# The last two batches' channel layers in one 2x2 block scheme with seven products

## The chip, the cores and the metric

The kernel runs on one core of one Trainium2 chip. The metric is the device time of one launch in microseconds (us), the median of several runs. Engines are named as the profile names them: PE is the matrix engine (PEld its weight load), DVE the vector engine, ACT the scalar engine, POOL the GpSimd engine, SP the engine whose queue issues most DMAs.

## The reference

Eight batches, twelve heads, 448 rows, head size 64. Cosine attention feeds a token mixer and a channel mixer:

```python
q_n = q / (norm(q) + 1e-06); k_n = k / (norm(k) + 1e-06)
attn = softmax(q_n @ k_n.T / tau)               # per batch and head
x = (attn @ v) as (8, 448, 768)
h  = relu(x.T @ w_tok1) @ w_tok2                # 448 -> 256 -> 448, over rows
u  = x + h.T
h2 = relu(u @ w_ch1) @ w_ch2                    # 768 -> 1536 -> 768, over channels
out = u + h2
```

The channel layers are the two matrix products of the last but one line. They work row by row, so two batches of 448 rows are simply 896 rows under the same weights.

## The kernel before

Matrix operands are fp16, sums are fp32 in PSUM. The work is cut into 48 pairs of heads, six pairs for each batch. The main loop runs over the pairs `i`; its order is written out by hand and nothing reorders it. In one turn of the loop, called a segment here, PE does for pair `i` the scores (`score`, `score_rest`), for pair `i-1` the product with v (`pv_rest`, `pv`) and the first token layer (`tok1`), and for pair `i-2` the second token layer (`tok2`). ACT does the exponentials out of PSUM. DVE divides (`rec`, `x`), adds the residual (`u`), and reduces the squares (`ssq`). POOL squares, scales and casts the inputs that come next (`side`). SP issues loads, stores and two DMA transposes for each pair: `tpose_dma` for the scaled q and k of pair `i+2`, and `udma`, which turns `u16` into `ut`, the operand of the first channel layer.

The channel layers are cut into units on a list (`queue`). A unit of `m_ch1` is one 128-channel tile of the hidden layer: six matmuls of 448 columns into one PSUM bank, then one ACT relu into `gt`. A unit of `m_ch2` is twelve matmuls of 384 columns, one DVE add of `u16`, and stores. An even batch has 12 + 6 units, an odd one 12 + 8, since the last 64 rows of an even batch share a 128-row tile with the first 64 of the odd one. When the third pair of batch `b` comes up, `refill(b - 1)` puts the units of the batch before on the list, and `due` hands them out so that they spread over the next six segments. They fill PE's waits. After the last segment the rest of batch 6 runs, mixed with the last pair's steps, then all of batch 7.

PSUM has two pools: `ps` with two buffers of one bank (tag "b"), `ps2` with three buffers of two banks (tag "s"). A wait is set for each tile: a matmul into a tile waits for the readers of the tile, even where they read its other bank.

Of the kernel before, what the change touches and what calls it, by code (L numbers as in the profile page):

```python
# [7 lines left out]
FP32 = mybir.dt.float32  # L8
FP16 = mybir.dt.float16
AF = mybir.ActivationFunctionType  # L10
ALU = mybir.AluOpType
# [11 lines left out]
def kernel(  # L23
# [12 lines left out]
    nc = tc.nc  # L36

    B, H, S, E = q.shape
    D = H * E
    T = moe_w_tok1.shape[1]  # L40
    C = moe_w_ch1.shape[1]
    SC = 112
    NCH = S // SC
    DT = D // 128
    CT = C // 128
    TT = T // 128
    DH = 384
    NPAIR = H // 2
    NP_ALL = B * NPAIR
    HP = 3  # L50
# [12 lines left out]
    KC = 3  # L63
    KS = 2 * KC + 1
    QS = 2 * NCH
    MAIN = [(128 * m, 128 * (m + 1)) for m in range(3)]
# [3 lines left out]
    def windows(b):  # L70
        return EVEN if b % 2 == 0 else ODD

    def pieces(lo, hi):
        got = []
        while lo < hi:
            c = lo // SC
            end = min(hi, SC * (c + 1))
            got.append((c, lo - SC * c, end - SC * c))
            lo = end
        return got  # L80

    cst = ctx.enter_context(tc.tile_pool(name="cst", bufs=1))
    qkv = ctx.enter_context(tc.tile_pool(name="qkv", bufs=7))
    nrm = ctx.enter_context(tc.tile_pool(name="nrm", bufs=3))
    att = ctx.enter_context(tc.tile_pool(name="att", bufs=4))
    mix = ctx.enter_context(tc.tile_pool(name="mix", bufs=2))
    outp = ctx.enter_context(tc.tile_pool(name="outp", bufs=3))
    ps = ctx.enter_context(tc.tile_pool(name="ps", bufs=2, space=bass.MemoryType.PSUM))
    ps2 = ctx.enter_context(tc.tile_pool(name="ps2", bufs=3, space=bass.MemoryType.PSUM))

# [2 lines left out]
    ut = {}  # L93
    u16 = {}
    gts = {}

    def old(i):
        return i < OLD


    def load_first(a, src):
# [3 lines left out]
                          in_=src[0, g].rearrange("(p c) e -> p (c e)", c=NCH))  # L105
        return t

    def load_rows(i, nm, src, bufs):
        h0 = 2 * (i % NPAIR)
        if old(i):  # L110
            t = qkv.tile([SC, QS, E], FP32, name=f"{nm}f_{i}", tag=f"{nm}f", bufs=bufs)
            nc.sync.dma_start(
                out=t[:].rearrange("p (g c) e -> p g (c e)", g=2),
                in_=src[h0:h0 + 2].rearrange("g (p c) e -> p g (c e)", c=NCH))
            return t
        t = qkv.tile([128, 2 * KC, E], FP32, name=f"{nm}f_{i}", tag=f"{nm}f", bufs=bufs)
        nc.sync.dma_start(out=t[:].rearrange("p (g c) e -> p g (c e)", g=2),
                          in_=src[h0:h0 + 2, 0:128 * KC].rearrange("g (p c) e -> p g (c e)", c=KC))
        return t

    def load_rest(i, nm, src):
        h0 = 2 * (i % NPAIR)
        t = qkv.tile([128, HP, E], FP32, name=f"{nm}r_{i}", tag=f"{nm}r", bufs=4)
        for g in range(2):
            nc.sync.dma_start(out=t[64 * g:64 * g + 64],
                              in_=src[h0 + g:h0 + 2 * HP:2, 128 * KC:S].rearrange("j p e -> p j e"))
        return t
# [29 lines left out]
    wc1t = cst.tile([128, DT, C], FP16, name="wc1t")  # L157
    wc2t = cst.tile([128, CT, D], FP16, name="wc2t")
# [1 line left out]
    NV = 3  # L160
    vts = []
    for i in range(NV):
        vt = cst.tile([128, HP, QS, E + 2], FP16, name=f"vt{i}")
        nc.gpsimd.memset(vt[:, :, :, E:E + 2].rearrange("p g c e -> p (g c) e"), 1.0)
        vts.append(vt)
    pts = []
    for i in range(2):
        pt = cst.tile([128, QS * S + 64], FP16, name=f"pt{i}")
        nc.gpsimd.memset(pt[:, QS * S:QS * S + 64], 0.0)
        nc.gpsimd.memset(pt[96:128, KS * S:KS * S + 64], 0.0)  # L170
        pts.append(pt)
# [32 lines left out]

    kqs = [cst.tile([128, 2, NCH, 2, E], FP16, name=f"kq{i}") for i in range(4)]
    sqs = [cst.tile([128, 2 * QS, E], FP32, name=f"sq{i}") for i in range(3)]
    for kq in kqs:
        nc.vector.memset(kq[96:128, 1].rearrange("p c g e -> p (c g e)"), 0.0)  # L210

# [39 lines left out]
    def some(i, a0, a1):  # L251
        sl, np_ = lay(i)
        return max(np_[a0:a1]), slice(sl[a0].start, sl[a1 - 1].stop)

    def sums(i, a0=0, a1=2):
        n, sl = some(i, a0, a1)
        st = pipe[i]
        if "ssq" not in st:
            st["ssq"] = nrm.tile([128, 2 * QS], FP32, name=f"ssq_{i}", tag="ssq", bufs=4)
            st["rn"] = nrm.tile([128, 2 * QS], FP32, name=f"rn_{i}", tag="rn", bufs=4)  # L260
        nc.vector.tensor_reduce(out=st["ssq"][0:n, sl], in_=st["sq"][0:n, sl], axis=AXX.X, op=ALU.add)  # L261
# [158 lines left out]
    def tok2(i, pe=False, wide=False):  # L420
        st = pipe[i]
        b, pj = i // NPAIR, i % NPAIR
        if pj == 0:
            u16[b] = mix.tile([128, DT, 4, 128], FP16, name=f"u16_{b}", tag="u16", bufs=4)
            ut[b] = mix.tile([128, DT, 4, 128], FP16, name=f"ut_{b}", tag="ut")
        psU = (ps2 if wide else ps).tile([128, 4, 128], FP32, name=f"psU_{i}", tag="s" if wide else "b")
        for m, lo in enumerate(windows(b)):
            for tt in range(TT):
                nc.tensor.matmul(psU[:, m], w2t[:, tt, lo:lo + 128], st["rt"][:, tt],  # L429
                                 start=(tt == 0), stop=(tt == TT - 1))  # L430
        u = u16[b][:, pj]
        nc.vector.tensor_tensor(out=u, in0=psU[:], in1=st["x"][:], op=ALU.add)  # L432
        if not pe:
            udma(i)

    def udma(i):
        b, pj = i // NPAIR, i % NPAIR
        nc.sync.dma_start_transpose(out=ut[b][:, pj], in_=u16[b][:, pj].rearrange("p m d -> p (m d)"))

    def upose(i, n=1):  # L440
        b, pj = i // NPAIR, i % NPAIR
        psT = ps.tile([128, n, 4, 128], FP16, name=f"psT_{i}", tag="b")
        for j in range(n):
            for m in range(4):
                nc.tensor.transpose(psT[:, j, m], u16[b][:, pj + j, m], id16[:])
        nc.vector.tensor_copy(out=ut[b][:, pj:pj + n], in_=psT[:])
# [20 lines left out]
    ost = {}  # L467
# [40 lines left out]
    def ch1_units(b):  # L508
        return [(ns(S, DT), lambda wide, ct=ct: m_ch1(b, ct, wide)) for ct in range(CT)]

    def ch2_units(b):
# [6 lines left out]
        else:  # L518
            order = [(m, c) for m in range(3) for c in cuts]
            if b % 2:  # L520
# [2 lines left out]
        return [(ns(hi - lo, CT), lambda wide, m=m, lo=lo, hi=hi, st=st: m_ch2(b, m, lo, hi, st, wide))  # L523
                for m, (lo, hi, st) in order]

    queue = []
    fed = [0.0, 0.0]

    def unit(wide=False):
        if queue:  # L530
            t, fn = queue.pop(0)
            fn(wide)
            fed[0] -= t

    def due():
        return queue and fed[0] > queue[0][0] / 2

    KEPT = 6000.0

    def refill(b):  # L540
        new = ch1_units(b) + ch2_units(b)
        fed[1] = (sum(t for t, _ in new) - (KEPT if b == 0 else 0.0)) / (NPAIR + 1 if b == 0 else NPAIR)
        queue.extend(new)

    with tc.manual_schedule():
# [3 lines left out]
            name=nc.get_next_instruction_name(), act_func_set_id=ACT_SET_LN_EXP,  # L549
# [94 lines left out]
        i = NPAIR  # L644
# [43 lines left out]
        for i in range(NPAIR + 1, NP_ALL):  # L688
            b, pj = i // NPAIR, i % NPAIR
            for c in range(KC):  # L690
                score(i, c)
            if i == NPAIR + 1:
                upose(i - 4, 2)
                tok2(i - 2, pe=True)
                pv_wide(i - 1)
                upose_act(i - 2)
                x_wide(i - 1)
                sums(i + 2)
            else:
                pv_rest(i - 1)  # L700
                pv(i - 1, 0)
                pv(i - 1, 1)
            if i == NPAIR + 1:
                refill(0)
            elif pj == 2 and b > 1:
                refill(b - 1)
            side(i)
            fed[0] += fed[1]
            unit(True)
            if old(i):  # L710
                score(i, KC)
            else:
                score_rest(i)
            if i > NPAIR + 1:
                tok2(i - 2)
            if i + 1 < DMA_T0:
                tpose(i + 1)
            if due():
                unit(True)
            while due():  # L720
                unit()
            tok1(i - 1)
            if i + 3 < NP_ALL:
                sums(i + 3)
        last = NP_ALL - 1
        unit(True)
        pv_rest(last)
        pv(last, 0)
        pv(last, 1)
        unit(True)  # L730
        tok2(last - 1)
        unit(True)
        tok1(last)
        unit(True)
        unit(True)
        tok2(last)
        refill(B - 1)
        while queue:
            unit()


# [33 lines left out]
```

## Time and profile before

| | |
|---|---|
| median of 3 runs | 385.88 us (385.34 to 386.58) |
| span of the profiled execution | 383.4 us |
| what lies around the span, by the median | 385.88 - 383.4 = 2.5 us |
| PE busy | 371.3 us, 97% |
| DVE, ACT, POOL busy | 217.5, 227.8, 238.4 us |
| granted PE clock, mean | 0.993 |
| last PE work ends, span ends | 378.98, 383.4 us |

The profile comes from one execution. A busy PE includes matmuls that stream one behind the other, so what one costs is read from the distance between starts and not from its own row. "Idle before" is time in which an engine had nothing that it could start, and the name behind it is what ended that.

### The profile page before, as it was taken

To read this page: it belongs to the slowest core of one execution; us is meant where nothing else is said; L and a number is where in the kernel's file an instruction comes from. 1 tells how busy PE (TensorE), PEld (TensorE's weight loads), DVE (VectorE), ACT (ScalarE), POOL (GpSimd) and SP (SyncE) were. 2 spreads that over 40 slices of the span, in tenths; PEclk is the share of its full clock that TensorE was granted. 3 is DMA by queue.
4 is the path that set the end of the run, shared out by engine and by line. 5 is a ranking of instruction groups with operands and counts; after the bars stand their busy time and mean duration, and the time that the engine had idled before them with its cause. 6 is when DMAs were issued, how large, how long until landed. Compare 5 with 4: busy or idle time off the path is not lost.

```text
span 383.4 us, 10204 instructions
## 1 busy us (share of the span) xinstructions
PE 371.3 (97%) x4114; PEld 243.0 (63%) x4114; DVE 217.5 (57%) x519; ACT 227.8 (59%) x400; POOL 238.4 (62%) x384
## 2 busy tenths in 40 slices
PE   7798999999999999999999999999999999999995
PEld 6466666676666666666666666667666666665563
DVE  7889766776437575556536674557445673241041
ACT  6899887855666447746665457855675466602400
POOL 8999997979667587677667577678567732000000
PEclk9899999999999999999999999999999999999999
DMA  7999999978988988978797978967884844013022
GB/s 215 262 246 223 251 241 185 222 161 171 218 189 149 216 161 197 214 148 190 180 204 129 226 170 202 183 164 172 217 195 117 155 118 115 15 55 97 0 79 87
DMA packets 117023, 64.60 MB, mean 169 GB/s; under 512 B 73328, under 2 KB 113392, under 8 KB 116976
## 3 DMA queue, kind: packets, MB, share of 16 engines
q1 hardware_dynamic: 111008, 58.48, 68.7%
q0 software_dynamic: 5616, 5.21, 8.6%
q8 instruction: 32, 0.52, 0.7%
q10 hardware_dynamic: 352, 0.27, 0.2%
q14 instruction: 15, 0.12, 0.1%
HBM read 43.45 MB, written 11.01 MB: 142 GB/s over the span
## 4 chain that ended last, share of the span: by engine, by line
PE 89%; ACT 4%; DVE 4%; DMA 1%; issue 1%; ACTq 0%; DVEq 0%
PE psF L478 29%; PE psG L462 28%; PE psO L379 9%; PE psS L340 8%; PE psU L429 5%; PE psR L415 5%; ACT pt L341 3%; PE psQ L347 2%; DVE ssq L261 2%; PE psO L362 1%; PE psO L397 1%; PE pst L317 1%; ACT sq L243 1%; DMA qf<-in_q_dram 1%; DVE kq L293 1%
## 5 line engine op out<-in xcount | busy, mean ns | idle before, releaser
L341 ACT ACTIVATE pt<-psS 128x896 f16<-128x896 f32 (+1 forms) x156 | 132.5, 917 | 55.8 <-PE psS L340 55.8
L462 PE MATMUL psG<-ut,wc1t 128*128 128x448 f16 x576 | 116.6, 352 | 0.0
L478 PE MATMUL psF<-wc2t,gt 128*128 128x384 f16 (+2 forms) x684 | 116.2, 323 | 0.0
L465 ACT ACTIVATE gt<-psG 128x448 f16<-128x448 f32 x96 | 51.8, 540 | 61.6 <-PE psG L462 61.6
L478 PEld LDWEIGHTS <-gt 128*128 128x128 f16 x684 | 64.2, 98 | 38.0
L293 POOL TENSOR_TENSOR kq<-kf,rn 128x384 f16<-128x384 f32 (+1 forms) x47 | 42.2, 898 | 72.7 <-DVE rn L270 69.0
L462 PEld LDWEIGHTS <-wc1t 128*128 128x128 f16 x576 | 53.9, 98 | 44.2
L482 DVE TENSOR_TENSOR ost<-psF,u 128x384 f32<-128x384 f32 (+2 forms) x65 | 34.6, 532 | 57.3 <-PE psF L478 55.8
L261 DVE TENSOR_REDUCE ssq<-sq 128x15 f32<-128x960 f32 (+2 forms) x51 | 56.1, 1101 | 2.9 <-ACT sq L243 2.7
L418 DVE TENSOR_SCALAR rt<-psR 128x256 f16<-128x256 f32 x48 | 20.1, 418 | 58.6 <-PE psR L415 58.6
L293 POOL TENSOR_TENSOR kq<-qf,rn 112x512 f16<-112x512 f32 x45 | 47.0, 1044 | 3.0
L340 PE MATMUL psS<-qk 64*128 64x448 f16 x312 | 41.4, 356 | 3.1 <-DVE qk L319 2.4
L245 POOL TENSOR_TENSOR sq<-qf 112x512 f32<-112x512 f32 x39 | 40.5, 1039 | 0.0
L245 POOL TENSOR_TENSOR sq<-kf 128x384 f32<-128x384 f32 (+1 forms) x46 | 40.1, 872 | 0.0
L379 PE MATMUL psO<-vt,pt 128*128 128x65 f16 (+1 forms) x1024 | 39.1, 193 | 0.0
L383 DVE TENSOR_TENSOR x<-psO,rec 128x256 f16<-128x256 f32 x82 | 34.8, 425 | 2.8
L379 PEld LDWEIGHTS <-pt 128*128 128x128 f16 (+1 forms) x1024 | 34.2, 97 | 3.5 <-issue 0.9
L432 DVE TENSOR_TENSOR u<-psU,x 128x512 f16<-128x512 f32 x48 | 32.4, 674 | 4.2 <-PE psU L429 2.9
L415 PEld LDWEIGHTS <-w1t 128*128 128x128 f16 x384 | 25.0, 98 | 8.7 <-issue 2.1
L429 PEld LDWEIGHTS <-w2t 128*128 128x128 f16 x384 | 24.8, 98 | 7.6 <-issue 1.0
L429 PE MATMUL psU<-rt,w2t 128*128 128x128 f16 x384 | 29.3, 219 | 0.2 <-POOL w2t L193 0.2
L415 PE MATMUL psR<-x,w1t 128*128 128x128 f16 x384 | 29.3, 219 | 0.2 <-DVE u L432 0.2
(58 smaller groups left out, 287.6 us busy)
## 6 DMA issues: line engine op xcount, KB each, us to landing
qf<-in_q_dram SPq DMA_DIRECT2D x47, 224.0 KB, 4.3
kf<-in_k_dram SPq DMA_DIRECT2D x36, 192.0 KB, 3.8
vf<-in_v_dram SPq DMA_DIRECT2D x36, 192.0 KB, 3.7
vf<-in_v_dram SPq DMA_DIRECT2D x12, 224.0 KB, 8.2
out_dram<-ost SPq DMA_DIRECT2D x8, 336.0 KB, 3.4
kf<-in_k_dram SPq DMA_DIRECT2D x11, 224.0 KB, 8.1
wc1t<-in_moe_w_ch_dram POOLq DMA_DIRECT2D x4, 576.0 KB, 10.0
wc2t<-in_moe_w_ch_dram POOLq DMA_DIRECT2D x2, 1152.0 KB, 12.0
```

Source lines behind the costliest of these rows:

```text
L245: nc.gpsimd.tensor_mul(out=dst, in0=src, in1=src)
L261: nc.vector.tensor_reduce(out=st["ssq"][0:n, sl], in_=st["sq"][0:n, sl], axis=AXX.X, op=ALU.add)
L293: eng.tensor_tensor(out=kq[0:p, a, 0:n].rearrange("p c g e -> p g c e"), in0=st["kq"[a]][:].rearrange("p (g c) e -> p g c e", g=2), in1=_b ...
L340: nc.tensor.matmul(psS[:, hh, 0:S], qk[hb, c * n:c * n + 128], qm[hb], start=True, stop=True)
L341: nc.scalar.activation(out=pts[i % 2][0:n, 2 * S * c:2 * S * (c + 1)].rearrange("p (h s) -> p h s", h=2), in_=psS[0:n, :, 0:S], func=AF.Ex ...
L379: nc.tensor.matmul(psO[:, m, 0:E + 1], pts[i % 2][0:n, at:at + 128], vt[0:n, i % HP, nch * hh + c, 0:E + 1], start=(old(i) and c == 0), st ...
L383: nc.vector.tensor_tensor(out=st["x"][:, :, hh * E:(hh + 1) * E], in0=psO[:, :, 0:E], in1=_bcast_free(rec[:], E), op=ALU.mult)
L415: nc.tensor.matmul(psR[:, tt], w1t[:, w1[m], tt * 128:(tt + 1) * 128], st["x"][:, m], start=(m == 0), stop=(m == 3))
L429: nc.tensor.matmul(psU[:, m], w2t[:, tt, lo:lo + 128], st["rt"][:, tt], start=(tt == 0), stop=(tt == TT - 1))
L462: nc.tensor.matmul(psG[:, 0:S], wc1t[:, dt, ct * 128:(ct + 1) * 128], ut[b][:, dt].rearrange("p m s -> p (m s)")[:, lo:lo + S], start=(dt ...
L465: nc.scalar.activation(out=gt[:, ct, (b % 2) * S:(b % 2 + 1) * S], in_=psG[:, 0:S], func=AF.Relu)
L478: nc.tensor.matmul(psF[:, 0:hi - lo], gt[:, ct, at:at + 128], wc2t[:, ct, lo:hi], start=(ct == 0), stop=(ct == CT - 1))
```

## The change

Batches 6 and 7 (`B0`, `B1`) are taken off the list. Their channel layers run together after the last segment. Rows are split into two halves by batch in the first layer, and into row tiles in the second; the summed and the output dimension are halved too. Each layer is then a 2x2 by 2x2 block product, done with seven products and fifteen block sums instead of eight products (Winograd's form of Strassen's scheme).

- First layer: seven products `p1` to `p7`, each for three column groups `d`, six matmuls of 448 columns each. The sums of weight blocks are `s1w1`, `w(1,0)` in place and, on DVE, `s2w1`, `s4w1`; the sums of the inputs are `t1x` to `t4x` on DVE. Results are put together by DVE out of PSUM (`e16`, `e167`, and the results of `p3` and `p4`, called g3 and g4 in the prediction), by ACT copies (`e1`, `e5`), by POOL (`c22`), with relus on ACT and DVE (`relus`).
- Second layer: three groups of two row tiles, in each seven products of six matmuls of 384 columns, called `q1` to `q7`; sums of weights `t1w2` and `t2w2` on POOL, `t3w2` and `t4w2` on DVE; sums of the hidden layer in `fast_g` on DVE; results put together by ACT (`f1`, `f5`), DVE (`f16`, `f167`, the halves of `orow`) and POOL (`f1u`, `f16u`, `f5u`, half of `orow`). The shared 128-row tile is done in the plain way (`shared_rows`).
- The units of batch 5 are spread over ten segments instead of six, since no other units are left for the last segments.
- The pools are arranged anew so that their memory can be released and taken by the new tiles (`early.close()`, `late.close()`). The last pair's `ut` is made by PE (`upose`) instead of by DMA.

The core of the diff:

```diff
+        segs = NPAIR + 1 if b == 0 else 10 if b == B - 3 else NPAIR
...
-            elif pj == 2 and b > 1:
+            elif pj == 2 and 1 < b < B - 1:
                 refill(b - 1)
...
+            if i == NP_ALL - 3:
+                early.close()
+                tail = ctx.enter_context(tc.tile_pool(name="tail", bufs=1, side="right", reuse_waits="tile"))
+            if i >= NP_ALL - 2:
+                fast_weights1(i - NP_ALL + 2)
         last = NP_ALL - 1
-        unit(True)
+        while queue:
+            unit(True)
+        fast_weights1(2)
+        gts[B0 // 2] = mix.tile([128, CT, 2 * S], FP16, name=f"gt_{B0 // 2}", tag="gt", bufs=1)
         pv_rest(last)
         pv(last, 0)
         pv(last, 1)
-        unit(True)
+        p1(0)
         tok2(last - 1)
-        unit(True)
+        p1(1)
         tok1(last)
-        unit(True)
-        unit(True)
-        tok2(last)
-        refill(B - 1)
-        while queue:
-            unit()
+        fast_x(1, 0, HD)
+        p2(0)
+        p2(1)
+        fast_x(2, 0, 1)
+        tok2(last, pe=True)
+        late.close()
+        tail2 = ctx.enter_context(tc.tile_pool(name="tail2", bufs=1, reuse_waits="tile"))
+        fast_weights2(1)
+        p1(2)
+        fast_x(2, 1, 2)
+        upose(last)
+        fast_x(2, 2, 3)
...
+        p5(0)
+        p2(2)
+        p6(0)
+        p6(1)
+        p7(0)
+        c22(0)
+        fast_weights2(2)
+        p3(0)
+        p4(0)
+        p7(1)
...
+        p5(1)
+        c22(1)
...
+        p6(2)
+        relus(0)
+        p3(1)
+        fast_weights2(3)
+        p4(1)
+        p7(2)
...
+        p5(2)
+        c22(2)
+        relus(1)
+        q1(0)
+        fast_weights2(4)
+        p3(2)
+        fast_g(0, 0, 4)
+        p4(2)
+        relus(2)
+        fast_g(0, 4, HC)
+        shared_rows(0, DH, None)
+        for g in range(3):
+            if g:
+                q1(g)
+            q5(g)
+            q6(g)
+            if g < 2:
+                fast_g(g + 1, 0, HC)
+            q2(g)
+            q7(g)
+            q3(g)
+            q4(g)
+        shared_rows(DH, D - 128, 0)
+        shared_rows(D - 128, D, D - 128)
```

and of the new functions those that the prediction speaks of:

```python
def q5(g):
    yz[g] = ps2.tile([128, 2, 512], FP32, name=f"psYZ_{g}", tag="s")
    prod2(5, g, yz[g][:, 1, 0:DH], True)
    nc.scalar.activation(out=etile2("f5", g), in_=yz[g][:, 1, 0:DH], func=AF.Copy)

def q6(g):
    prod2(6, g, yz[g][:, 0, 0:DH], True)
    tt(nc.vector, etile2("f16", g), yz[g][:, 0, 0:DH], eo["f1", g][:], ALU.add)
    ...
def q7(g):
    prod2(7, g, yz[g][:, 0, 0:DH], False)
    tt(nc.vector, etile2("f167", g), yz[g][:, 0, 0:DH], eo["f1", g][:], ALU.add)
    ...
def q3(g):
    prod2(3, g, yz[g][:, 1, 0:DH], False)
    tt(nc.vector, orow[g][0][:, DH:D], yz[g][:, 1, 0:DH], eo["f16u", g][:], ALU.add)
    ...
def q4(g):
    prod2(4, g, yz[g][:, 0, 0:DH], False)
    ...
```

## The prediction

> **What bounds the kernel now.** I read the page first (busy shares, slices, the chain that ended last), then the busy time by windows over the last stretch, then the timeline and the groups by form for durations.
>
> ```profile
> PE 371.3 (97%) x4114; PEld 243.0 (63%) x4114; DVE 217.5 (57%) x519; ACT 227.8 (59%) x400; POOL 238.4 (62%) x384
> ...
> PE   7798999999999999999999999999999999999995
> ...
> PE 89%; ACT 4%; DVE 4%; DMA 1%; issue 1%; ACTq 0%; DVEq 0%
> PE psF L478 29%; PE psG L462 28%; PE psO L379 9%; PE psS L340 8%; PE psU L429 5%; PE psR L415 5%; ACT pt L341 3%; PE psQ L347 2%; DVE ssq L261 2%; PE psO L362 1%; PE psO L397 1%; PE pst L317 1%; ACT sq L243 1%; DMA qf<-in_q_dram 1%; DVE kq L293 1%
> ```
>
> The chain is PE and 57% of the span is the channel layers (L478, L462): fewer matmuls there are worth their whole time, as long as PE does not wait.
>
> ```profile
> core 0: us, PE busy (x) PEld busy (x) DVE busy (x) ACT busy (x) POOL busy (x), PEclk, DMA share, GB/s
> ...
> 318.73:326.00 7.27, 7.27 (x81) 4.55 (x79) 2.24 (x6) 5.09 (x9) 0.55 (x2) 1.00 0.57 129
> ...
> 349.56:363.18 13.62, 13.62 (x74) 7.04 (x72) 0.56 (x1) 5.97 (x11) 0.00 (x0) 1.00 0.10 30
> 363.18:378.98 15.80, 15.80 (x109) 10.04 (x107) 5.43 (x10) 0.54 (x1) 0.00 (x0) 1.00 0.26 76
> ```
>
> In the last two windows (batch 7) PE never waits and the others are nearly idle. The change fills them with block sums. So the question is whether PE can still run through.
>
> **What goes.** The first of these windows is 72 matmuls of 448 columns: 13.62/72 = 0.189 us each. The chain in order of time has 12 of 384 columns as pieces of 1.95 us: 0.1625 each. The first layer goes from 144 to 7x3x6 = 126 matmuls: -18 x 0.189 = -3.4. The second goes from 168 to 7x3x6 + 12 (the shared tile) + 12 (cut in both kernels) = 138 full ones: by 384-column work, 27.3 us before against 126 x 0.1625 + 3.9 = 24.4 after: -2.9. Four transposes of the last pair come to PE: +0.3. Sum **-6.0 us** of PE.
>
> **The segments.** Without batch 6's units the last ten segments hold 2.75 us of attention and on average 2.9 us of units, 5.7 in place of about 7.2. POOL needs per segment 0.83+0.72+1.04 (scales), 0.5 (cast), 0.83+0.29+1.04 (squares) = 5.25. Following scores, `ssq`, `rn`, scales and the transpose (lands in 3.1 us), only pair 45's transpose comes out about 0.2 us late. I take +0.5, bounds 0 and 3 (POOL 5.25 against two short segments of 5.0).
>
> **The prices of the new work.** Durations by form:
>
> ```profile
> L432 DVE TENSOR_TENSOR u<-psU,x 128x512 f16<-128x512 f32 x48 | 32.4, 674 | 4.2 <-PE psU L429 2.9
> L482 DVE TENSOR_TENSOR ost<-psF,u 128x384 f32<-128x384 f32 x47 | 25.3, 539 | 40.2 <-PE psF L478 39.0 <-DMA vf<-in_v_dram 1.3
> L319 DVE COPY qk<-pst 128x896 f16<-128x896 f16 x10 | 5.9, 589 | 0.2 <-PE pst L317 0.2
> L319 DVE COPY qk<-pst 128x224 f16<-128x224 f16 x2 | 0.5, 274 | 0.1
> L245 POOL TENSOR_TENSOR sq<-qf 112x512 f32<-112x512 f32 x39 | 40.5, 1039 | 0.0
> L245 POOL TENSOR_TENSOR sq<-kf 128x384 f32<-128x384 f32 x36 | 29.7, 826 | 0.0
> ```
>
> DVE out of PSUM: 1.04 ns an element + 0.14, so 896 take 1.07. DVE in fp16: the copies give 0.5 ns + 0.16, so 2304 take 1.33, 1792 (`relus`) 1.07, 768 take 0.55. No row has an fp16 add of two SBUF tiles; the other bound is the fp32 rate, 2.5 us for 2304. I take the copy, all 16-bit as these are. POOL: 1.66 ns + 0.19, so 2304 take 4.0, 896 take 1.68. ACT: 0.92 for 896, 0.49 for 384. PE's end reaches DVE or ACT after 0.2 us (psG to relu, 350.70 to 350.90), DVE's end reaches PE after 0.06 (copy to psS, 8.31 to 8.37).
>
> DVE and POOL also get in each other's way:
>
> ```profile
> 9.29 1.06 POOL L245 TENSOR_TENSOR sq<-kf 112x512 f32<-112x512 f32 x1
> ...
> 10.04 1.64 DVE L293 TENSOR_TENSOR kq<-qf,rn 112x512 f16<-112x512 f32 x1
> 10.28 0.81 POOL L190 DMA_DIRECT2D w2n<-in_moe_w_tok_dram  x1
> 11.12 1.45 POOL L293 TENSOR_TENSOR kq<-kf,rn 112x512 f16<-112x512 f32 x1
> ...
> 14.40 0.69 DVE L293 TENSOR_TENSOR kq<-qf,rn 112x512 f16<-112x512 f32 x1
> 14.44 1.55 POOL L293 TENSOR_TENSOR kq<-kf,rn 112x512 f16<-112x512 f32 x1 [0.31 <-DVE rn L270]
> ```
>
> The same DVE operation, two SBUF inputs, takes 0.69 alone and 1.64 when it comes behind POOL's; POOL's takes 1.04 alone and 1.55 behind DVE's. The second waits out the first. The Trainium skill ("SBUF — State Buffer", Who interferes with whom) states this as a rule that speaks against the change: POOL shares a port pair with DVE, the lock is held for the whole instruction, and a DVE operation with two SBUF inputs blocks against it; it adds `tensor_scalar` in its two-port mode, so `relus`. No run here shows it for one-input operations.
>
> In the sum I let `relus` (one SBUF input) be held too, by the nearest row, the two-input one; if it is not, the sum is 1.5 smaller. Without any hold it is 2.5 smaller.
>
> **Where PE waits** (t = 0: last psF of the queue ends; `pv(47)` follows to 0.99).
>
> *Start.* DVE ends two adds of that psF at 1.3 (0.2 + 1.12) and then has `s4w1` ahead of the `x` of pair 47. POOL's `t1w2` (4.0) waits for `pv(47)` and is free at 1.2. `tok2(46)` needs a "b" buffer that this `x` frees. If `s4w1` is first: 1.3 + 1.33 + 0.6 = 3.3, while PE is there at 2.1: 1.2 lost. If `t1w2` is first, `s4w1` starts at 5.2 and PE loses 5.1. A tenth of a us decides, finer than rows tell: I take 3.2 between the two.
>
> *First layer*, clock c from the end of `e167(0)`. POOL: `c22(0)` to 1.7, `t2w2` to 5.7, `c22(1)` to 7.4. DVE has g3(0), g4(0), `e167(1)`, `e16(2)` to 5.9 as PE delivers, then `relus(0)`, held off to 7.4, to 8.5, g3(1) to 9.6. It frees the bank of `p5(2)`, which PE reached at 8.1: 1.6 lost. DVE goes on without a pause: `t3w2` 10.9, g4(1) 12.0, `e167(2)` 13.1, `relus(1)` 14.1, `t4w2` 15.5, g3(2) 16.5, ACT's relu on it 17.5. PE is through `p4(2)` and two thirds of the shared tile at 15.5 and waits for that relu: 2.1 lost. Then four sums of `fast_g` with 0.6 behind POOL's `c22(2)` to 18.8, g4(2) 19.9, `relus(2)` 21.0: 3.1 lost. With 0.7 of small waits 7.5. DVE is the bound here: about 21 us of work against PE's 15.
>
> *Second layer.* `psYZ` is one tile with two banks, and in the built order each product waits for the reader of the one before, though that is in the other bank. In each group: `q6` waits for the copy `f5` of `q5` (0.2 + 0.49 + 0.06 = 0.75); `q3` waits for `f167` of `q7` (0.2 + 0.54 + 0.06 = 0.8); `q4` waits for the add after `q3` (0.8). That is 2.35, three times 7.05. In groups 0 and 1 `f167` stands in DVE's queue behind `f16`, four sums of 768 (2.2) and the add after `q2`: 0.2 + 0.54 + 2.2 + 3 x 0.54 less the 1.95 in which PE does `q2` and `q7` is 2.1 instead of 0.8, so +2.6 for both. Sum 9.7. If POOL's `f16u` and `f5u` (0.83 each) get between the sums, 3.3 more.
>
> *End.* Two half adds instead of one after the last matmul, and three big stores close together: +0.5 (bounds 0 and 1.5).
>
> Off PE's path: `s1w1` and `w(1,0)` on POOL (8 us after pair 47's transpose, needed 10 us later), `t1x` to `t4x` (done within 0.5 us of need, so the cover is thin), the fp32 copies on ACT.
>
> **Sum.** -6.0 + 0.5 + 3.2 + 7.5 + 9.7 + 0.5 = +15.4; rows of DVE that follow each other overlap by some 0.07 us, about 20 times on these chains: -1.4. So **+14.0**: span 383.4 + 14.0 = 397.4, and with the 2.5 us around it **399.9 us**.
>
> Two prices of the Trainium skill ("VectorE: DVE Perf Modes", What auto-detection actually checks): 16-bit two-input operations run two elements a cycle, as I took them, and a 16-bit single-input one in SBUF four, which would make `relus` 0.6 instead of 1.07 and the sum 1.3 smaller. No row here shows either.
>
> **Rivals.**
> 1. *Fp16 sums at the fp32 rate* (only fp32 rows have two inputs). `s4w1`, `t3w2`, `t4w2` +1.2 each, `relus` +0.9 each, `fast_g` +0.4 for 768: about +5 in the first layer, +3.2 in the second, +2 to 3 in the start: 411. Against it: the 16-bit copies. Chance 0.09.
> 2. *PE runs through: faster.* The seven-for-eight saving stays whole if every reader is done before PE comes back to its tile. Place: `q6`, `q3`, `q4`, which each wait for an evacuation of 0.75 to 0.8 us with no other matmul between. It decides if these nine waits and the wait on DVE before `q5(0)` together stay under 6 us; by the rows they are 12 to 17. If the tile waits cost nothing and POOL did not block: 385.9 - 6.0 + 3 = 383. Chance 0.04; within 0.3% 0.02.
> 3. *Thin segments.* POOL (5.25) and the transposes become the bound over the last ten pairs and add 3 to what stands above: 403. For it: POOL's 62% at 7.2 us a segment. Against: the two chains meet within 0.2 us. Chance 0.1.
> 4. *No hold between DVE and POOL, and `s4w1` first*: -2.0 - 2.5, so 395.4. For it: the hold is seen three times only, on fp32. Against: each time it is whole. Chance 0.15.
>
> My own case has 0.6. The granted clock was 1.00 in every window above, with PE never idle; what a wait of 3 us and more does to it no row shows, so it is left to the range. The range takes in cases 3 and 4 and most of 1: **391 to 410**. A measurement of this kernel can tell about 0.3% (1.2 us) from no change. Faster 0.04, same 0.02, slower 0.94.
>
> **What would show it.** Right: PE near 75% busy in the last 30 us, idle before psYZ matmuls put down to DVE and ACT, some 0.75 us each and over 2 us twice; DVE over 90% busy through the first layer; POOL rows of about 4 us with stretched DVE rows beside them. A single step is wrong if PE has no gap before `q6`, if 2304 fp16 elements take over 2 us on DVE, or if PE waits in the segments. The forecast is wrong if PE's waits after the last segment stay under 6 us.

## The result, and the profile after

The changed kernel takes 409.17 us (median of 4 runs, 407.84 to 410.47) against 386.02 of the kernel before beside it (385.34 to 386.58): a ratio of 1.061, interval 1.058 to 1.064. The forecast was 399.9 with a range of 391 to 410. The direction held, and the range did by 0.8 us; the number was 9.3 us too low. The profiled execution of the changed kernel is its longest one: 410.47 us, span 408.6, so 1.9 us lie around the span. It is 1.3 us above the median, so the terms below add up to more than the medians differ.

The page after, in the same lines as before (engines, PE's slices with the granted clock, the chain):

```profile
PE 375.3 (92%) x4082; PEld 241.7 (59%) x4082; DVE 255.5 (63%) x569; ACT 228.5 (56%) x394; POOL 277.3 (68%) x403
...
PE   7789999989999999999999999997999989946684
...
PEclk9999999999999999999999999999999999987878
...
PE 73%; DVE 8%; DMA 7%; POOL 5%; ACT 3%; issue 3%; DVEq 0%; ACTq 0%; POOLq 0%
```

PE has 32 matmuls fewer and yet is busy 4 us longer, and its share of the chain falls from 89 to 73%. Both show in the last five slices: PE's share falls to 4 to 8 tenths there, and the granted clock, which was 9 to the end before, to 7 to 8.

The same stretch by windows (the steps around the last pair; first layer in two parts; the three groups of the second layer):

```profile
core 0: us, PE busy (x) PEld busy (x) DVE busy (x) ACT busy (x) POOL busy (x), PEclk, DMA share, GB/s
325.38:337.34 11.96, 10.85 (x104) 6.45 (x104) 10.26 (x21) 5.50 (x6) 5.75 (x1) 1.00 0.26 68
337.34:350.57 13.23, 13.09 (x67) 6.43 (x66) 10.03 (x10) 2.80 (x4) 8.13 (x3) 1.00 0.00 0
350.57:363.43 12.86, 7.48 (x37) 3.56 (x37) 12.65 (x16) 3.29 (x4) 5.19 (x3) 0.95 0.01 2
363.43:376.60 13.17, 8.86 (x38) 4.27 (x36) 6.52 (x11) 0.49 (x1) 3.33 (x3) 0.76 0.09 28
376.60:391.49 14.89, 10.53 (x43) 5.11 (x42) 5.87 (x9) 0.98 (x2) 4.24 (x4) 0.73 0.18 53
391.49:401.60 10.11, 8.03 (x44) 4.34 (x43) 2.79 (x5) 0.98 (x2) 3.68 (x4) 0.93 0.18 53
```

In the second half of the first layer DVE is busy 12.65 of 12.86 us and PE 7.48: DVE is the bound there. In the groups no engine is busy for more than four fifths, so they are bound by waiting for each other. PE's waits after the last segment, by what it waited for (us in total, times, longest):

```profile
PE psYZ L667 <- DVE f L535: 6.7, 3, 3.0
PE psF_shared L732 <- ACT gt L622: 3.1, 1, 3.1
PE psYZ L667 <- DVE orow L535: 2.2, 3, 0.7
PE psYZ L667 <- ACT f L690: 1.9, 3, 0.6
PE psF_shared L732 <- DVE gt L630: 1.7, 1, 1.7
PE psU L433 <- DVE x L387: 1.1, 1, 1.1
PE psY L585 <- DVE e L535: 0.5, 1, 0.5
```

All 10.8 us on psYZ are waits of the kind that the prediction named. How one of 3.0 us comes about is in the chain of group 0, in order of time (start, length, what):

```profile
365.93 1.15 PE psYZ L667 x6
...
367.17 0.56 DVE f L535
367.73 0.47 DVE s1g L535
368.20 0.02 issue
368.23 1.15 DVE s2g L535
369.38 1.18 DVE s3g L535
370.56 0.47 DVE s4g L535
371.04 0.47 DVE orow L535
371.50 0.47 DVE f L535
371.98 0.04 issue
372.02 1.79 PE psYZ L667 x6
```

`q6` ends, DVE adds `f16`, then makes four sums for the next group and the add of `q2`, and only then `f167` (the second "DVE f"). `q3` waits for that add, since it writes the other bank of the same tile. And `q3` itself takes 1.79 us, where six matmuls at full clock take 1.14: the granted clock fell to 0.50 about 0.6 us after its start and stayed there for 6.3 us. Rows of PE from this stretch:

```profile
362.61 0.82 PE L732 MATMUL psF_shared<-wc2t,gt 128*128 128x384 f16 x2 [1.72 <-DVE gt L630]
363.22 2.13 PE L667 MATMUL psYZ<-t1w,s1g 128*128 128x384 f16 x6
...
386.61 2.08 PE L667 MATMUL psYZ<-wc2t,s4g 128*128 128x384 f16 x6 [3.00 <-DVE f L535]
```

The second of these is `q5` of group 0. It is slow too (clock 0.50), behind the two waits in the shared tile, 3.08 and 1.72 us.

Where the 408.6 - 383.4 = 25.2 us of span went. The first column is the prediction's term, the second is the trace: a stretch's length less its matmuls at full clock, or less the same stretch before. PE's work is counted as in the prediction, since products at full clock cost what they did (six matmuls of 448 columns start 1.13 us apart, of 384 columns 0.97).

| | predicted | trace |
|---|---|---|
| PE's work | -6.0 | -6.0 |
| the first 90 us | 0 | +0.9 |
| last ten segments | +0.5 | +2.4 |
| start, to the first `p6` | +3.2 | +1.4 |
| first layer, 26.1 us for 18.8 of matmuls | +7.5 | +7.3 |
| second layer, 38.2 us for 19.5 of matmuls | +9.7 | +18.7 |
| end | +0.5 | +0.5 |
| rows that overlap | -1.4 | (in the rows above) |
| sum | +14.0 | +25.2 |

The 0.9 us is no part of the change: the profiled execution of `split_late` below, the same program up to there, runs level with the kernel before, and that of `deferral` is 2.0 us late by then. Of the second layer's 18.7 us, the windows give 4.31 + 4.36 + 2.08 = 10.75 as time without a matmul, which leaves 7.9 us. Of these some 1.5 us belong to the nine waits: the last matmul before a wait has none behind it, and a row of six lasts 1.14 us where the next row in a stream starts after 0.97. So from start to start the waits are 12.2 us, and about 6.4 us are matmuls made slower by the clock, 1.0 of them in `q5` of group 0, before any wait on psYZ.

### The profile page after: what moved, and what is told of

It reads as the page before. It is cut to its first block, busy times and chain, and to the rows that moved or that the text cites. A ratio compares the mean times of both kernels' runs of the same rounds, so it can differ in the third digit from the quotient of the medians.

```text
span 408.6 us, 10255 instructions
## 1 busy us (share of the span) xinstructions
PE 375.3 (92%) x4082; PEld 241.7 (59%) x4082; DVE 255.5 (63%) x569; ACT 228.5 (56%) x394; POOL 277.3 (68%) x403
## 4 chain that ended last, share of the span: by engine, by line
PE 73%; DVE 8%; DMA 7%; POOL 5%; ACT 3%; issue 3%; DVEq 0%; ACTq 0%; POOLq 0%
PE psG L466 19%; PE psF L482 18%; PE psO L383 8%; PE psS L344 7%; PE psYZ L667 5%; PE psU L433 4%; PE psR L419 4%; DMA qk<-kq 3%; DMA ut<-u 3%; POOL kq L297 3%; ACT pt L345 2%; PE psQ L351 1%; PE psY L585 1%; PE psX L585 1%; POOL sq L249 1%
## 5 line engine op out<-in xcount | busy, mean ns | idle before, releaser
L466 PE MATMUL psG<-ut,wc1t 128*128 128x448 f16 x432 | 89.0, 352 | 0.1
L482 PE MATMUL psF<-wc2t,gt 128*128 128x384 f16 x504 | 88.1, 326 | 0.0
L482 PEld LDWEIGHTS <-gt 128*128 128x128 f16 x504 | 47.2, 98 | 28.1
L466 PEld LDWEIGHTS <-wc1t 128*128 128x128 f16 x432 | 39.9, 98 | 31.8 <-issue 0.4
L469 ACT ACTIVATE gt<-psG 128x448 f16<-128x448 f32 x72 | 38.8, 538 | 30.3 <-PE psG L466 30.3
L486 DVE TENSOR_TENSOR ost<-psF,u 128x384 f32<-128x384 f32 (+1 forms) x48 | 25.7, 535 | 27.7 <-PE psF L482 26.4
```

Source lines behind the costliest of these rows:

```text
L466: nc.tensor.matmul(psG[:, 0:S], wc1t[:, dt, ct * 128:(ct + 1) * 128], ut[b][:, dt].rearrange("p m s -> p (m s)")[:, lo:lo + S], start=(dt ...
L469: nc.scalar.activation(out=gt[:, ct, (b % 2) * S:(b % 2 + 1) * S], in_=psG[:, 0:S], func=AF.Relu)
L482: nc.tensor.matmul(psF[:, 0:hi - lo], gt[:, ct, at:at + 128], wc2t[:, ct, lo:hi], start=(ct == 0), stop=(ct == CT - 1))
```

## The experiments

The theory to test: the second layer loses by waits for a whole tile, by the order on DVE's queue, and by the clock that falls in those waits; the first layer is bound by DVE; the rest is the price of taking batch 6 off the list. Rivals: POOL's hold on DVE explains most; or the deferral does. The kernels before took 385.4 to 386.3 us (medians) beside these runs; ratios are to them.

### Two tiles in place of one (`split`)

```diff
-        yz[g] = ps2.tile([128, 2, 512], FP32, name=f"psYZ_{g}", tag="s")
+        yz[g] = [ps2.tile([128, 2, 512], FP32, name=f"ps{k}_{g}", tag="s") for k in ("Zo", "Yo")]
```

> The change with psYZ taken apart: q5 and q3 in one PSUM tile, q6, q7 and q4 in another; nothing else. Theory (tile-wide waits, then the granted clock that falls in them): the waits before q6 (0.58 to 0.64 us) and before q3 (3.0) go; q4 now waits for f167, which still stands behind the four sums, about 2.4 us in groups 0 and 1 and nothing in group 2. Waits in the second layer 5 instead of 11 us, clock there over 0.85: time 398 (395 to 401). Rival A (DVE held by POOL is the bound of the second layer, whatever the tiles): f16, sums and adds are just as late, the wait moves whole to q4 and to the next group: 406 to 410. Rival B (products of 1.9 us are slow for another reason than waits, such as DVE and POOL traffic): waits fall by 6, rows stay at 0.49 us each: 402 to 404.

398.94 us, ratio 1.035 (1.031 to 1.039). The waits before `q6` and `q3` are gone; `q4` waits 1.40 and 2.03 us for `f167`, nothing in group 2. The theory's number was 398; the waits that stayed are somewhat shorter than I expected. The work and its order on DVE and POOL are the same, so 10 us were the price of one tile with two banks, the clock lost in its waits included.

### `f167` ahead of the sums (`split_late`)

```diff
-            if g < 2:
-                fast_g(g + 1, 0, HC)
             q2(g)
             q7(g)
+            if g < 2:
+                fast_g(g + 1, 0, HC)
```

> As the run with psYZ taken apart, and the sums of the next group moved behind q7, so that f167 is ahead of them on DVE. Theory: q4 finds f167 done, the second layer has under 2 us of waits (q5 or q6 of the next group may wait for a sum for some tenths), the clock stays near 1.00: time 391.5 (389.5 to 394). Rival A (DVE is the bound): adds of q3 and q4 now come behind the sums and buffers come free late: 398 or more. Rival B (rows slow for another reason): 398 to 400.

394.59 us, 1.022 (1.018 to 1.027), a little outside the range given. In its profiled execution, its shortest, the three groups are (windows as above):

```profile
361.57:368.56 6.99, 6.99 (x37) 3.93 (x36) 4.23 (x9) 0.49 (x1) 2.83 (x3) 0.83 0.00 0
368.56:375.43 6.87, 6.87 (x44) 4.10 (x42) 5.17 (x10) 0.98 (x2) 3.80 (x5) 1.00 0.37 115
375.43:382.38 6.95, 6.95 (x45) 4.11 (x43) 4.72 (x9) 0.98 (x2) 3.88 (x5) 1.00 0.37 116
```

20.8 us in place of 38.2, PE without a pause. DVE is busy 4 to 5 of 7 us: it was never the bound of the second layer, its order was. The 0.83 of group 0 is left over from the waits in the shared tile, which are still there (3.1 and 1.7 us).

### Idle matmuls in the waits (`kept_busy`)

```diff
+            hold(g, 0.6)
             q6(g)
...
+            hold(g, 2.4 if g < 2 else 0.6)
             q3(g)
+            hold(g, 0.6)
             q4(g)
```

> The change with idle matmuls of the unit matrix into a spare PSUM tile where PE waits in the second layer: 0.6 us before q6, 2.4 before q3 (0.6 in group 2), 0.6 before q4. They do no work of the reference. Theory (waits lower the granted clock, which then makes the next products slow): rows of the products stay at 0.33 us, windows of the three groups at a clock over 0.9, 6 us less: 403 (401 to 405). Rival (products are slow for another reason, or the clock falls without regard to idle time): 409 to 411, the matmuls filling waits only.

405.58 us, 1.052 (1.050 to 1.055): faster than the change with 165 matmuls more on PE, which is the plainest proof that the clock was lost. The windows of its three groups:

```profile
363.29:375.48 12.19, 11.54 (x104) 8.20 (x103) 6.73 (x12) 0.49 (x1) 3.34 (x3) 0.86 0.01 4
375.48:387.14 11.66, 10.98 (x109) 7.90 (x108) 5.88 (x9) 0.98 (x2) 4.25 (x4) 1.00 0.23 69
387.14:396.52 9.38, 9.15 (x77) 6.06 (x75) 2.79 (x5) 0.98 (x2) 3.70 (x4) 1.00 0.29 86
```

33.2 us instead of 38.2. All but the first two products, behind the shared tile's waits, run at full clock. I had expected 403, and 405 at most: the idle matmuls took longer than the waits that they filled (44 of them 2.6 us, with 0.55 of waiting left behind them), so part was given back.

### Without POOL's adds between the sums (`no_hold`)

```diff
-        tt(nc.gpsimd, j3(etile2("f16u", g)), j3(eo["f16", g][:]), urow(TILES[g][0], 1), ALU.add)
-        tt(nc.gpsimd, j3(etile2("f5u", g)), j3(eo["f5", g][:]), urow(TILES[g][1], 1), ALU.add)
```

> The change without POOL's f16u and f5u, that is without the residual in the right half of the output rows of the three groups; DVE adds f16 and POOL adds f5 in their place. It takes away what gets between the sums s1g to s4g in the change (s2g 1.15 and s3g 1.26 us instead of 0.55). Theory A (POOL holds DVE for its whole operation, and the granted clock halves only after waits of about 3 us): s2g and s3g take 0.55, the wait before q3 falls from 3.0 to 1.7 in groups 0 and 1, and the products behind it run at full clock: 2.6 us of waits and about 5 of clock, 401.5 (400 to 404). Theory B (the hold alone counts, the clock falls after waits of 1.7 too): 406 to 407. Rival (DVE is slow there whatever POOL does): 409.

This kernel leaves the residual out of the right half of the groups' rows. 403.09 us, 1.044 (1.040 to 1.048): theory A's case. In the change POOL's two adds stand beside `s2g` (1.15 us in the chain above) and `s3g`:

```profile
367.81 1.16 POOL L535 TENSOR_TENSOR f16u<-f,u 128x384 f32<-128x384 f32 x1 [8.69 <-DVE f L535]
...
368.93 1.22 POOL L535 TENSOR_TENSOR f5u<-f,u 128x384 f32<-128x384 f32 x1
369.31 1.26 DVE L535 TENSOR_TENSOR s3g<-gt 128x768 f16<-128x768 f16 x1
```

From the timeline of `no_hold`, the same two sums and the two products `q3` that waited 3.0 us in the change:

```profile
369.50 0.56 DVE L535 TENSOR_TENSOR s2g<-s1g,gt 128x768 f16<-128x768 f16 x1
369.98 0.55 DVE L535 TENSOR_TENSOR s3g<-gt 128x768 f16<-128x768 f16 x1
...
371.98 1.14 PE L667 MATMUL psYZ<-wc2t,s4g 128*128 128x384 f16 x6 [1.42 <-DVE f L535]
...
382.26 1.14 PE L667 MATMUL psYZ<-wc2t,s4g 128*128 128x384 f16 x6 [1.68 <-DVE f L535]
```

Two waits shorter by 1.3 and 1.6 us gave 6 us in all, since the products behind them take 1.14 us (a row of six at full clock) and no longer 1.8 to 2.1. Between the two profiled executions the waits on psYZ are 3.2 us less (7.6 for 10.8) and the clock's share about 4 us less (2.2 for 6.4). It is not gone: group 0 still starts at 0.50 (363.0 to 368.6 us), behind the shared tile's waits, in `q5`, `q6` and a part of `q2`. So the hold is real, and it counts more by the clock than by itself.

### The deferral alone, and spread out (`deferral`, `spread`)

`deferral` runs plain products, batch 6 deferred as in the change. `spread` is the same with the list dealt out over more segments:

```diff
-        segs = NPAIR + 1 if b == 0 else 10 if b == B - 3 else NPAIR
+        segs = NPAIR + 1 if b == 0 else 8 if b == B - 4 else 10 if b == B - 3 else NPAIR
+        todo = queue if b >= B - 4 else new
```

> No seven-product scheme: plain products, but the units of batch 6 are taken out of the last segments and done at the end with those of batch 7, with the pools laid out as in the change. Theory: this alone costs what the trace of the change shows ahead of its first product, 0.9 us at the start and 2.4 in the thin segments: 389.3 (388 to 391), psS waiting for transposes in the last ten segments, granted clock 1.00 at the end. Rival (the thin segments are slow because POOL and DVE make weight sums there too): 386 to 387. Rival (the deferral is most of the loss): over 395.

> As the run of the deferral alone (plain products), but the units of batches 4 and 5 are handed out evenly over the last 16 segments (3.4 us in each instead of 4.5 in six and 2.9 in ten). Theory (a segment under about 5.3 us is too short for POOL and the transpose, so psS waits for qk): segments of 6.1 us each, no wait of psS over 0.3 us: 387.3 (386 to 388.5) against 389.9. Rival (the cost of the deferral lies elsewhere, in the pools or the end): 389 to 390.5.

`deferral`: 389.86 us, 1.011 (1.008 to 1.014), 4.5 us above before, in the range and a little above the number expected. `spread`: 386.86 us, 1.0024 (1.0005 to 1.0042). The waits of the scores for the transposes in the changed kernel:

```profile
277.67 0.74 PE L344 MATMUL psS<-qk 64*128 64x448 f16 x6 [0.73 <-DMA qk<-kq]
285.26 0.74 PE L344 MATMUL psS<-qk 64*128 64x448 f16 x6 [1.38 <-DMA qk<-kq]
```

`deferral` has two such waits (2.5 us), `spread` none. So the segments are short only because the units were dealt out unevenly; about 3 of the 4.5 us were this (2.5 in the trace, 3.0 between the two medians).

### Weight sums out of the first layer (`weights_late`)

```diff
         p3(1)
-        fast_weights2(3)
...
         q1(0)
-        fast_weights2(4)
...
         fast_g(0, 4, HC)
+        fast_weights2(3)
+        fast_weights2(4)
```

> As split_late, and the weight sums t3w2 and t4w2 moved on DVE from the middle of the first layer to behind the last sums of fast_g(0). Theory (DVE is the bound of the first layer; these two took 2.23 and 3.23 us there, part of it held by POOL): the waits in the shared tile (3.1 and 1.7 us) shrink to under 1 in all, some 1.3 come back in group 0, where f16 stands behind them: 391 (389.5 to 392.5) against 394.6. Rival (the waits in the shared tile are the latency of the last products' readers, or POOL's c22): as before, 394 to 395.5.

391.11 us, 1.013 (1.011 to 1.016), a time as the theory had it. The kernel has the changes of `split_late` too. PE's waits after the last segment:

```profile
PE psF_shared L732 <- DVE gt L630: 2.2, 1, 2.2
PE psYo L667 <- DVE f L535: 1.8, 1, 1.8
PE psU L433 <- DVE x L387: 1.1, 1, 1.1
```

The wait of 3.1 us for the relu is gone, and 1.8 came back in group 0 where 1.3 were expected. The wait for `relus(2)` did not shrink as expected (2.2 for 1.7 before): DVE still had the sums of `fast_g(0, 0, 4)` ahead of it in the queue. So the waits became only 1.3 us less than in `split_late` (5.1 for 6.4 in all). As much again came from the clock: group 0 ran at 1.00 and no longer at 0.83, worth 1.2 us. Together that is the 2.5 us by which the two profiled executions differ from the last ten segments on; the medians are 3.5 apart, and the rest is not explained.

### All of it, and the tie at the start (`mended`)

`mended` joins these steps and makes `s4w1` right behind `s2w1`.

> The whole change with all that the runs pointed at: products in separate tiles, sums behind f167, t3w2 and t4w2 late, units of batches 4 and 5 spread over 16 segments, and s4w1 right behind s2w1, in the last segment, so that the x of pair 47 is not behind it. Theory (these are the whole of the loss): 387.5 (386 to 389.5), the six us of PE saved and as many still lost. Rival 1 (nothing else is in the way): 384, faster than before. Rival 2 (with the waits gone here they come back elsewhere): over 390.

395.72 us, 1.026 (1.023 to 1.029): rival 2, and most of it (4.3 of the 4.6 us above `weights_late`) has one reason. First the change, then `mended`:

```profile
326.66 1.36 DVE L535 TENSOR_TENSOR s4w<-wc1t,s2w 128x2304 f16<-128x2304 f16 x1
326.67 5.75 POOL L535 TENSOR_TENSOR t1w<-wc2t 128x2304 f16<-128x2304 f16 x1 [5.72 <-issue]
```
```profile
325.68 4.53 POOL L535 TENSOR_TENSOR t1w<-wc2t 128x2304 f16<-128x2304 f16 x1 [3.65 <-issue]
325.78 5.65 DVE L535 TENSOR_TENSOR s4w<-wc1t,s2w 128x2304 f16<-128x2304 f16 x1
```

The operation that starts second is held until the first is through: POOL's 4.53 became 5.75, DVE's 1.36 became 5.65. In the change DVE was first by 0.01 us and PE lost 1.08; here POOL was first by 0.10 us, the `x` of pair 47 stood behind, and PE waited:

```profile
PE psU L433 <- DVE x L387: 5.4, 1, 5.4
```

The list also ran dry before the last pair (PE waited 1.1 us for `rt`). The early start that I meant for `s4w1` did not come about: with the list spread, `s2w1` before it began at 324.4 us and not at 318.3 as in `split_late`.

### Is there a version that is faster? (`second_only`, `retimed`, `end_moved`)

`second_only` keeps the first layer plain. `retimed` is the whole change with every step put where the traces showed DVE and POOL idle, and with the list spread but 6 us of it kept for the last pair:

```diff
         fast_x(2, 2, 3)
+        fast_weights2(2)
+        fast_weights1(3)
...
-            tt(nc.vector, t[k][:, j0:j1], a, b, ALU.subtract)
+            tt(nc.gpsimd if k == 4 and j0 == 2 else nc.vector, t[k][:, j0:j1], a, b, ALU.subtract)
...
+        fast_weights2(3)
         p6(2)
...
         p3(2)
-        fast_g(0, 0, 4)
         p4(2)
         relus(2)
-        fast_g(0, 4, HC)
+        fast_g(0, 0, HC)
+        fast_weights2(4)
```

> Only the second layer of the last two batches by seven products; the first layer plain, batch 6's in the segments and batch 7's at the end. Weight sums in the last two segments, products in separate tiles, the group of batch 6 between the last pair's steps, the sums of the second group while PE does batch 7's first layer. Theory (a saving survives where the sums lie beside other work of PE): 2.9 us of PE saved, 0.3 of transposes and 0.5 of end added, waits under 1: 383.7 (382.5 to 385) against 385.4. Rival (sums and adds on DVE delay the x, rt and u of the last pair): 386 to 389.

> The whole change, nothing left out, with the order of its steps made anew from the traces of the runs so far: as split_late; units of batches 4 and 5 spread over 16 segments with 6 us of them kept for the last pair; s4w1 on DVE behind the last t3x, where DVE idled 1.7 us; the last t4x on POOL and t2w2 right behind it, before c22(0); t3w2 before e16(2), where DVE idled 1.1 us; relus(2) ahead of the sums of group 0, and t4w2 and the adds of the shared tile behind them. Theory (what is lost is order on DVE and POOL, not work): against weights_late 391.1, the start gives 1.1 (tok2(46) finds its x), the segments 2.3, the shared tile 1.8, group 0 1.6: 384.3 (383 to 386.5) against 386 of before. Rival (DVE has too much to do beside the first layer, each wait that goes comes back elsewhere): 387 to 390.

> As retimed, with two changes. The last columns of the shared tile come before q3 and q4 of the last group, so that the last thing is q4 in pieces of 256 and 128 columns, one add each, stored by columns. And relus(0) stands behind g3(1) on DVE, so that p5(2) finds its bank free. Theory (PE was 1.3 us ahead of before at its last matmul in retimed and lost it in the last adds and stores, 5.7 us there against 4.4): 1.0 from the end and 0.7 from p5(2): 384.3 (383.5 to 385.5), faster than before by 0.3 to 0.6%. Rival (the last stores take their time whatever stands before them): 385.5 to 386.5, no difference from before.

`second_only`: 388.01 us, 1.005 (1.003 to 1.007), its rival's case: `t3w2` and `t4w2` stood ahead of the last `x`, and the waits around the last pair add to 1.7 us. `retimed`: 385.96 us, 0.9996 (0.998 to 1.001), no difference from before. All of PE's waits from the short segments to the end:

```profile
PE psZ L587 <- DVE gt L535: 0.6, 1, 0.6
PE psS L344 <- DMA qk<-kq: 0.5, 2, 0.3
PE psF_shared L740 <- DVE gt L632: 0.3, 1, 0.3
PE psYo L669 <- DVE f L535: 0.2, 1, 0.2
```

23 us came back with nothing left out. Why it is not faster still: of the 6.0 us saved, these waits take 1.6; the first 50 us took 0.6 longer in this execution; starts of neighbouring rows lie up to 0.3 us further apart than their matmuls need wherever PE turns to a tile that was just released (six matmuls from 337.84 to 339.19, 1.35 us for 1.13), some 2 us over the two layers by my estimate; and the end takes 5.7 us after PE's last row instead of 4.4. PE is done 1.3 us earlier than before and loses it in the last adds and stores. `end_moved` took the wait on psZ away (none there any more) and put the shared tile ahead of the last products, but the last stores then stand close together, the end is 6.2 us after PE's last row, and the waits for the transposes were 1.1 us for 0.5: 386.21 us, 1.002 (0.999 to 1.005). With that the saving is spent.

## Why the prediction was right, and where it was not

Right: the direction, and the mechanism. PE's waits were put at nine places in the second layer, at the shared tile and at the start, and each is there.

- *Second layer, the step that failed* (9.7 predicted, 18.7 measured). Two terms. First, the clock: "what a wait of 3 us and more does to it no row shows, so it is left to the range". It was worth about 6.4 us of the 9.0 that were missing. `kept_busy` and `no_hold` show it from both sides. The Trainium skill has a price ("TensorE: Matmul & The Clock Gate", Part 1: The HAM clock gate): half the clock after an idle window of about 3.4 us, full again after as long a busy one. The trace agrees in kind and not in size: 3.0 us were enough, and the clock was 0.50 from 372.6 to 378.9, that is for 6.3 us. The sum held two waits of about 2.1, so the page would not have decided it; with the "3.3 more" that stands behind the sum they become about 3.7 each, and it would have. Second, that POOL's `f16u` and `f5u` get between the sums was named and left out of the sum. They did (1.15 and 1.26 us in place of 0.55), and the wait before `q3` became 3.2 instead of 2.1, counted as in the prediction from the end of a product at full clock (the profile's 3.0 starts 0.17 later). Without the adds it is 1.6 and 1.8 (`no_hold`: 1.42 and 1.68 in the profile). The small waits, counted alike, came out as 0.75 to 0.88 for 0.75 to 0.8. In all the waits were 12.2 us for 9.7.
- *Two sums as printed.* The one for the wait before `q3` has a 0.54 too many, as it adds up to 2.6; the 2.1 is right for the operations named. The 138 full matmuls of the second layer are without the cut ones; the 24.4 us has those too.
- *First layer* (7.5 and 7.3). The total is right by luck, since its parts are not. `p5(2)` lost 0.2 and not 1.6: `relus(0)` got in between `t2w2` and `c22(1)` on POOL. The relu wait was 3.1 and not 2.1: `t4w2` took 3.23 us behind `c22(2)`, which I had not seen. The wait for `relus(2)` was 1.7 and not 3.1. Too large and too small cancelled. That DVE is the bound is shown by its 12.65 busy us of 12.86, and by `weights_late`, where the wait for the relu went with two of its sums.
- *Start* (3.2 and 1.4): a middle between 1.2 and 5.1 that neither case could give. The two cases are right to 0.3 us: 1.08 in the change, 5.36 in `mended`.
- *Segments* (0.5 and 2.4). That start and segments nearly cancel, -1.8 and +1.9, is luck as well. I reckoned with a mean segment of 5.7 us. Some are 4.7 to 5.0, shorter than POOL's 5.25, and those set the transposes. Rival 3, with 3 us more, was closer in size.
- *Prices.* DVE's fp16 sums of 2304 took 1.36 us for the 1.33 taken from the copy, `relus` 0.61 for 1.07, POOL's 2304 in fp16 4.5 for 4.0. `relus`, with one SBUF input, are held too: 1.42 us behind POOL in the change, 0.61 alone. The rules of the Trainium skill that the prediction weighed both fit here: two and four elements a cycle ("VectorE: DVE Perf Modes", What auto-detection actually checks) with these 1.36 and 0.61 us, and the lock for `tensor_scalar` ("SBUF — State Buffer", Who interferes with whom) with the 1.42 us.
- *Rivals.* Fp16 sums at fp32 rate: wrong by the rows. PE running through: not in this order; `retimed`, with another one, comes near it (1.6 us of waits from the short segments on) and is still not faster. No hold: wrong.

## What to carry to other kernels

A product scheme that trades matmuls for sums is worth only what its sums leave of PE: count each sum on the queue where it will stand, and each reader of a PSUM tile by the tile and not by the bank. Price every predicted wait twice, once as itself and once as the clock that it may cost. Work that is deferred to the end must be replaced evenly in the segments that it leaves, or their transfers become the wait.

## What the runs showed of the hardware

- After each wait of 3.0 us on psYZ the granted clock was 0.50 for 6.3 us. It need not fall within the wait: after 3.08 us in the shared tile two matmuls still ran at 1.00, and it was 0.50 after the next wait of 1.72 us. Standing alone, waits of 1.42 and 1.68 us (`no_hold`) left it at full. In between it went both ways: half after 2.03 us in `split` (0.90 over the first 1.1 us, 0.54 over the next 3.5), full after 2.16 and 1.79 in `weights_late` (1.00). What decides there was not tried.
- A hold between DVE and POOL lasts for the whole first operation, but two operations of POOL one behind the other do not keep it: DVE's `s2g` ended 0.41 us after `f16u`, while `f5u` behind it was stretched from 0.91 (group 2) to 1.22 us. Which of two starts first was decided by 0.01 and 0.10 us in two kernels, and was worth 4.3 us (a wait of 1.1 or of 5.4).
